# Linear attention, 32 heads: the order of the first and last heads and of the loads, and three stores split unevenly over the DMA engines

## The chip, the cores and the metric

The kernel runs on one core of a Trainium2 chip. The metric is the device time of one execution in microseconds (us), lower is better; where several executions are given it is their median.

A core has five instruction streams: PE (matrix multiplication), DVE (elementwise, reads PSUM and SBUF), ACT (activation functions), POOL (elementwise, SBUF only) and SP (here it only issues DMAs). Sixteen DMA engines carry all transfers between HBM and SBUF. A DMA is split over the engines, and each engine that has done its part adds to the DMA's semaphore.

## The reference

```
phi_q = where(q > 0, q + 1, exp(q)) + 1e-6
phi_k = where(k > 0, k + 1, exp(k)) + 1e-6
kv  = einsum("bhsd,bhse->bhde", phi_k, v)
z   = einsum("bhsd->bhd", phi_k)
num = einsum("bhqd,bhde->bhqe", phi_q, kv)
den = einsum("bhqd,bhd->bhq", phi_q, z)[..., None] + 1e-6
out = num / den
```

q, k, v and out are bfloat16 of shape 1 x 32 x 2048 x 128: 32 heads, each with 512 KB of q, of k, of v and of out, 67.1 MB in all.

## The kernel before

The heads are independent. The 2048 rows of a head lie over 128 partitions, 16 rows (of 128 numbers) to a partition, so that one partition holds 4 KB of a head's q, k, v or out. phi is taken apart as min(exp(x), 1) + 1e-6 plus max(x, 0), and each part has its own matrix multiplication. The steps of head h, by the names that the order lists use (a number behind the point is the part of the head):

- `ldk`, `ldq`, `ldv`: loads into one of seven buffers (`NI = 7`); all are issued by SP but `ldv0`, which ACT issues. A load waits until the steps that read its buffer for head h-7 are done.
- `ek` (ACT) takes exp of k; `em` (DVE) limits it; `rkp` (POOL) is max(k, 0), for half of head 0 `rkd` on DVE. `v1` (POOL) copies v beside a column of ones, so that the sum z comes out of the same multiplication.
- `kv` (PE) is 32 matmuls into one PSUM area; `kvs` (DVE) copies the result to SBUF, and `kv` of the next head waits for that.
- `T` (PE) transposes q into PSUM; `eq` (ACT) takes exp, `emq` (DVE) limits it, `rqa` (ACT) and `rqb` (DVE) take max(q, 0), one half each. There is one PSUM area for the transposes, so `T` of the next head waits for `eq`, `rqa` and `rqb`.
- `n` (PE) multiplies phi_q with kv in two groups of tiles (12 and 4); `r` (DVE) is the reciprocal of the denominator, `f` (DVE) multiplies and writes bfloat16 to one of twelve output buffers (`NO = 12`), `a` (DVE) adds 1e-6 to the denominator of the second group.
- `st` (SP) stores a head, and that of head 31 in three parts. `f` of head h waits for `st` of head h-12, whose buffer it takes.
- `w0` to `w16` are matmuls on the identity matrix without a use of their results, which keep PE busy in the beginning. `ones`, `eps0` to `eps2`, `v1ones0`, `v1ones1` fill constants; `exp` (ACT) runs the activation once.

Nothing is scheduled at run time. Each engine runs its instructions in the order of a list written out by hand (`ORDER`, one string for each engine), and the class `Program` derives from the dependencies which semaphores each instruction waits for. SP's list is therefore also the order in which loads and stores stand in the queue of the DMA engines. An instruction that waits holds up everything behind it in its list.

A load of head 1 and later goes through `wide`, which describes the HBM side as 32 rows of 16 KB; a store goes through `dma_start` with 128 rows (partitions) of 4 KB, so that each of the 16 DMA engines moves 8 rows. The lines of the profile that matter: 344 and 349 loads, 453 stores, 361 `ek`, 364 `em`, 371 `rkp`, 375 `v1`, 382 `kv`, 387 `kvs`, 394 `T`, 398 `eq`, 400 `emq`, 404 `rqa`, 407 `rqb`, 423 and 425 `n`, 438 `a`, 441 `r`, 445 `f`, 330 warm-ups.

Of the kernel before, what the change touches and what calls it, by code (L numbers as in the profile page):

```python
# [6 lines left out]
P = 128  # L7
# [4 lines left out]
NI, NO, NE, NR, NV, NQ, NK = 7, 12, 2, 2, 2, 2, 2  # L12
WARM = (1, 1, 1, 1, 1, 1, 1, 1, 1, 1, 1, 1, 1, 1, 1, 1, 12)
HALVES = ((0, 8), (8, 16))
WHOLE = ((0, 16),)
# [47 lines left out]

def st_parts(h):
    return ((0, 6), (6, 12), (12, 16)) if h == NH - 1 else WHOLE
# [22 lines left out]
def rqb_parts(h):  # L88
    if na(h) == 16:
        return ()  # L90
    if h == NH - 1:
# [6 lines left out]
        w16 w6 w7 w8 w9 w10 w2 T0.0 w0 w11 w12 w5 w13 w1 T0.1 w14 kv0.0 kv0.1 w3 w15 w4 T1.0 kv1.0 n0.0 n0.1  # L98
# [10 lines left out]
        v1ones0 eps0 v1ones1 ones rkd0.0 em0.0 em0.1 emq0.0 em1.0 eps1 rqb0.0 eps2 emq0.1 kvs0 em2.0 kvs1 rqb1.0  # L109
        r0.0 f0.0 emq1.0 em3.0 a0.1 kvs2 r0.1 rqb2.0 f0.1 r1.0 emq2.0 f1.0 em4.0 a1.1 r1.1 rqb3.0 f1.1 r2.0 kvs3  # L110
        f2.0 emq3.0 em5.0 a2.1 r2.1 rqb4.0 f2.1 r3.0 kvs4 f3.0 emq4.0 em6.0 a3.1 r3.1 rqb5.0 f3.1 r4.0 kvs5 f4.0
# [13 lines left out]
        r27.1 rqb29.0 f27.1 r28.0 kvs29 f28.0 emq29.0 em31.0 a28.1 r28.1 rqb30.0 f28.1 r29.0 kvs30 f29.0 emq30.0  # L125
        emq31.0 a29.1 r29.1 emq31.1 f29.1 emq31.2 kvs31 r30.0 f30.0 a30.1 r30.1 f30.1 r31.0 f31.0 a31.1 r31.1
# [12 lines left out]
        ident0 ident rkp0.0 rkp1.0 v10.0 v10.1 v11.0 rkp2.0 v12.0 rkp3.0 v13.0 rkp4.0 v14.0 rkp5.0 v15.0 rkp6.0  # L139
        v16.0 rkp7.0 v17.0 rkp8.0 v18.0 rkp9.0 v19.0 rkp10.0 v110.0 rkp11.0 v111.0 rkp12.0 v112.0 rkp13.0 v113.0  # L140
        rkp14.0 v114.0 rkp15.0 v115.0 rkp16.0 v116.0 rkp17.0 v117.0 rkp18.0 v118.0 rkp19.0 v119.0 rkp20.0 v120.0
        rkp21.0 v121.0 rkp22.0 v122.0 rkp23.0 v123.0 rkp24.0 v124.0 rkp25.0 v125.0 rkp26.0 v126.0 rkp27.0 v127.0
        v128.0 rkp28.0 rkp29.0 v129.0 rkp30.0 v130.0 rkp31.0 v131.0
    """,
    "SP": """
        ldk0.0 ldq0.0 ldk1.0 ldk2.0 ldv1.0 ldq1.0 ldv2.0 ldk3.0 ldq2.0 ldv3.0 ldk4.0 ldq3.0 ldv4.0 ldv5.0 ldq4.0
        ldk5.0 ldk6.0 ldv6.0 ldq5.0 ldq6.0 ldk7.0 ldk8.0 st0.0 ldv7.0 ldv8.0 ldq7.0 ldk9.0 ldv9.0 st1.0 ldv10.0
        ldq8.0 ldk10.0 ldq9.0 ldk11.0 st2.0 ldq10.0 ldq11.0 ldv11.0 st3.0 ldk12.0 ldk13.0 ldv12.0 ldq12.0
        ldv13.0 ldv14.0 ldq13.0 ldk14.0 ldq14.0 ldv15.0 st4.0 ldk15.0 ldv16.0 ldk16.0 ldq15.0 st5.0 ldq16.0
        ldv17.0 ldk17.0 st6.0 ldq17.0 ldv18.0 ldk18.0 st7.0 ldk19.0 ldv19.0 ldq18.0 ldq19.0 st8.0 ldk20.0  # L150
        ldk21.0 ldv20.0 ldk22.0 st9.0 ldq20.0 ldv21.0 ldq21.0 st10.0 ldv22.0 ldk23.0 ldq22.0 ldk24.0 st11.0
        ldv23.0 ldk25.0 ldq23.0 st12.0 ldv24.0 ldq24.0 ldv25.0 st13.0 ldk26.0 ldq25.0 ldv26.0 st14.0 ldk27.0
        ldq26.0 ldv27.0 st15.0 ldk28.0 ldv28.0 ldq27.0 st16.0 ldk29.0 ldq28.0 ldv29.0 st17.0 ldq29.0 ldk30.0
        ldv30.0 st18.0 ldq30.0 ldk31.0 st19.0 ldq31.0 st20.0 ldv31.0 st21.0 st22.0 st23.0 st24.0 st25.0 st26.0
        st27.0 st28.0 st29.0 st30.0 st31.0 st31.1 st31.2
# [13 lines left out]
class Program:  # L169
# [10 lines left out]
    def add(self, eng, key, fn, deps=(), dma=None, inc=True):  # L180
        assert key not in self.op, key
        self.op[key] = (eng, fn, tuple(deps), dma, inc)
# [71 lines left out]
def bass_standalone__linear_attn_elu__prompt_kernel(nc: bass.Bass, q: bass.AP, k: bass.AP, v: bass.AP, out: bass.AP):  # L254
    B, H, S, D = q.shape
    assert D == P and S == 16 * P and B * H == NH
    NT = S // P
# [5 lines left out]
    qf, kf, vf, of = (t.rearrange("b h s d -> (b h) s d") for t in (q, k, v, out))  # L263
    rows = lambda t, h: t[h].rearrange("(p j) d -> p j d", j=NT)

    with ExitStack() as es:
# [70 lines left out]

        def wide(e, to, of):
# [13 lines left out]
        def head(h):  # L352
# [99 lines left out]
            for i, (a, b) in enumerate(st_parts(h)):  # L452
                add("SP", f"st{h}.{i}", lambda e, a=a, b=b: e.dma_start(rows(of, h)[:, a:b], o_sb[:, h % NO, a:b]),
                    [f"f{h}.{j}" for j, (t0, nb, m, b0) in enumerate(groups(h)) if t0 < b and a < t0 + nb * m],
                    dma=f"o{h % NO}")
# [43 lines left out]
```

## Time and profile before

| | |
|---|---|
| median of 3 runs | 169.06 us (169.06 to 169.13) |
| the profiled execution | 169.27 us |
| its span, first to last instruction | 168.0 us |
| mean granted TensorE clock | 0.991 |
| busy: PE, DVE, ACT, POOL | 156.5, 151.9, 149.7, 93.2 us |
| moved by DMA | 67.51 MB, 402 GB/s over the span |
| read from HBM, written | 50.33 MB, 16.78 MB |

The profile comes from one execution. Its time is the span and 1.27 us around it. Times in its rows are counted from the span's start. A row of the timeline reads: start, duration, engine and line, operation, what is written and what is read, how many instructions, and in brackets how long the engine was idle before and what ended that. In the rows of the stretches a busy time stands behind each engine, with the number of instructions in brackets; the DMA share is the mean busy share of the 16 DMA engines. A row of DMA issues ends with the median time from issue to landing. Beside the views, the trace holds every DMA packet (start, duration, bytes, queue; not which of the 16 engines moved it) and the time of every increment of a DMA's semaphore.

### The profile page before, as it was taken

To read this page: it belongs to the slowest core of one execution; us is meant where nothing else is said; L and a number is where in the kernel's file an instruction comes from. 1 tells how busy PE (TensorE), PEld (TensorE's weight loads), DVE (VectorE), ACT (ScalarE), POOL (GpSimd) and SP (SyncE) were. 2 spreads that over 40 slices of the span, in tenths; PEclk is the share of its full clock that TensorE was granted. 3 is DMA by queue.
4 is the path that set the end of the run, shared out by engine and by line. 5 is a ranking of instruction groups with operands and counts; after the bars stand their busy time and mean duration, and the time that the engine had idled before them with its cause. 6 is when DMAs were issued, how large, how long until landed. Compare 5 with 4: busy or idle time off the path is not lost.

```text
span 168.0 us, 6186 instructions
## 1 busy us (share of the span) xinstructions
PE 156.5 (93%) x2716; PEld 150.8 (90%) x2716; DVE 151.9 (90%) x300; ACT 149.7 (89%) x102; POOL 93.2 (55%) x71
## 2 busy tenths in 40 slices
PE   6967999999999999999999999999999989999940
PEld 2456999999999999999999999999999989999840
DVE  0339799999999999999999999999999989999992
ACT  3499899999999999999999999999999979995800
POOL 1397676555555666665555556666655356642000
PEclk9999999999999999999999999999999999999996
DMA  5999999999999999999999999999999999999985
GB/s 207 433 418 414 394 425 386 421 416 410 414 410 425 402 410 396 429 405 431 395 425 419 409 414 430 407 415 419 421 419 423 404 421 436 397 421 409 401 329 216
DMA packets 9819, 67.51 MB, mean 402 GB/s; under 512 B 2080, under 2 KB 2464, under 8 KB 6816
## 3 DMA queue, kind: packets, MB, share of 16 engines
q1 hardware_dynamic: 9648, 66.59, 96.8%
q8 instruction: 21, 0.34, 0.8%
q10 hardware_dynamic: 144, 0.52, 0.8%
q14 instruction: 6, 0.05, 0.1%
HBM read 50.33 MB, written 16.78 MB: 400 GB/s over the span
## 4 chain that ended last, share of the span: by engine, by line
DVE 74%; PE 15%; DMA 4%; issue 3%; ACT 1%; SPq 0%
DVE la L445 36%; DVE la L400 10%; DVE la L364 10%; DVE la L407 9%; PE la L382 7%; DVE la L441 4%; DMA la<-in_k_dram 4%; DVE la L387 3%; PE la L423 3%; PE la L394 3%; PE la L425 3%; DVE la L438 2%; ACT la L361 1%; ACT la L398 1%; SPq L349 0%
## 5 line engine op out<-in xcount | busy, mean ns | idle before, releaser
L371 POOL TENSOR_SCALAR la<-la 128x2048 bf16<-128x2048 bf16 (+1 forms) x32 | 59.9, 1873 | 55.2 <-PE la L382 44.9
L445 DVE TENSOR_TENSOR la<-la 128x1536 bf16<-128x1536 f32 (+2 forms) x65 | 77.7, 1196 | 0.1
L423 PE MATMUL la<-la 128*128 128x129 bf16 x512 | 67.0, 219 | 0.2 <-DVE la L387 0.2
L425 PE MATMUL la<-la 128*128 128x129 bf16 x512 | 67.0, 219 | 0.0
L382 PE MATMUL la<-la 128*128 128x129 bf16 x1024 | 63.3, 220 | 2.0 <-POOL la L375 1.4
L361 ACT ACTIVATE la<-la 128x2048 bf16<-128x2048 bf16 (+1 forms) x33 | 61.3, 1859 | 4.3 <-DMA la<-in_k_dram 4.3
L398 ACT ACTIVATE la<-la 128x2048 bf16<-128x2048 bf16 (+2 forms) x35 | 60.2, 1730 | 4.4 <-PE la L425 2.7
L382 PEld LDWEIGHTS la<-la 128*128 128x128 bf16 x1024 | 59.3, 98 | 2.5 <-issue 1.7
L425 PEld LDWEIGHTS la<-la 128*128 128x128 bf16 x512 | 49.5, 97 | 0.0
L423 PEld LDWEIGHTS la<-la 128*128 128x128 bf16 x512 | 47.9, 97 | 0.4 <-DVE la L387 0.4
L375 POOL COPY la<-la 128x1024 int32<-128x1024 int32 (+1 forms) x33 | 34.1, 1037 | 5.9 <-DMA la<-in_v_dram 5.9
L394 PE MATMUL la<-la 128*128 128x128 bf16 x512 | 34.0, 219 | 1.3 <-DVE la L387 0.9
L404 ACT ACTIVATE la<-la 128x1024 bf16<-128x1024 bf16 (+1 forms) x32 | 33.5, 1046 | 0.0
L394 PEld LDWEIGHTS la<-la 128*128 128x128 bf16 x512 | 29.9, 98 | 2.7 <-DVE la L387 1.0
L400 DVE TENSOR_SCALAR la<-la 128x2048 bf16<-128x2048 bf16 (+2 forms) x35 | 24.0, 687 | 4.5 <-ACT la L398 4.5
L364 DVE TENSOR_SCALAR la<-la 128x2048 bf16<-128x2048 bf16 (+1 forms) x33 | 23.7, 718 | 1.1 <-ACT la L361 1.1
L418 PE MATMUL la<-la 128*128 128x3 bf16 (+1 forms) x128 | 21.6, 168 | 1.3 <-DVE la L445 1.3
L407 DVE TENSOR_SCALAR la<-la 128x1024 bf16<-128x1024 bf16 x31 | 20.5, 661 | 0.0
L441 DVE RECIPROCAL la<-la 128x12 f32<-128x12 f32 (+2 forms) x65 | 13.0, 201 | 1.6 <-PE la L425 0.6
L418 PEld LDWEIGHTS la<-la 128*128 128x128 bf16 x128 | 12.5, 98 | 1.5 <-DVE la L445 1.5
L330 PE MATMUL la<-la 128*128 128x480 bf16 x28 | 7.8, 428 | 1.5 <-POOL la L315 1.5
L387 DVE CAST la<-la 128x129 bf16<-128x129 f32 x32 | 7.7, 240 | 0.8 <-PE la L382 0.8
(16 smaller groups left out, 11.4 us busy)
## 6 DMA issues: line engine op xcount, KB each, us to landing
la<-in_k_dram SPq DMA_DIRECT2D x32, 512.0 KB, 19.6
la<-in_q_dram SPq DMA_DIRECT2D x32, 512.0 KB, 19.7
la<-in_v_dram SPq DMA_DIRECT2D x31, 512.0 KB, 19.6
out_dram<-la SPq DMA_DIRECT2D x31, 512.0 KB, 19.9
la<-in_v_dram ACTq DMA_DIRECT2D x1, 512.0 KB, 5.3
out_dram<-la SPq DMA_DIRECT2D x2, 192.0 KB, 2.7
out_dram<-la SPq DMA_DIRECT2D x1, 128.0 KB, 3.2
```

The lines of the kernel that those rows point to most:

```text
L361: add("ACT", f"ek{h}.{i}", lambda e, a=a, b=b: e.activation(em_sb[:, h % NE, a:b], k_sb[:, h % NI, a:b], ACT.Exp), over("ldk", h, ld_parts ...
L364: add("DVE", f"em{h}.{i}", lambda e, a=a, b=b: e.tensor_scalar(em_sb[:, h % NE, a:b], em_sb[:, h % NE, a:b], 1.0, EPS, op0=ALU.min, op1=AL ...
L371: add("POOL", f"rkp{h}.{i}", lambda e, a=a, b=b: e.tensor_scalar(rk_sb[:, h % NR, a:b], k_sb[:, h % NI, a:b], BIG, 0.0, op0=ALU.min, op1=A ...
L375: add("POOL", f"v1{h}.{i}", lambda e, a=a, b=b: e.tensor_copy(v1_sb[:, h % NV, a:b, 0:D].bitcast(i32), v_sb[:, h % NI, a:b].bitcast(i32)), ...
L382: ins = e.matmul(kv_ps, lhsT=src[:, j], rhs=v1_sb[:, h % NV, j, 0:NC], start=(j + part == 0), stop=(j == NT - 1 and part == 1))
L394: ins = e.transpose(xT[:, j], q_sb[:, h % NI, j], ident[:])
L398: add("ACT", f"eq{h}.{i}", lambda e, a=a, b=b: e.activation(emq_sb[:, h % NQ, a:b], xT[:, a:b], ACT.Exp), over("T", h, t_parts, a, b) + fr ...
L400: add("DVE", f"emq{h}.{i}", lambda e, a=a, b=b: e.tensor_scalar(emq_sb[:, h % NQ, a:b], emq_sb[:, h % NQ, a:b], 1.0, EPS, op0=ALU.min, op1 ...
L407: add("DVE", f"rqb{h}.{i}", lambda e, a=a, b=b: e.tensor_scalar(rq_sb[:, h % NQ, a:b], xT[:, a:b], 0.0, None, op0=ALU.max), over("eq", h, ...
L423: e.matmul(to, lhsT=emq_sb[:, h % NQ, t], rhs=kvs_sb[:, h % NK, 0:NC], start=late and c == 0, stop=False, skip_group_check=True)
L425: ins = e.matmul(to, lhsT=rq_sb[:, h % NQ, t], rhs=kvs_sb[:, h % NK, 0:NC], start=False, stop=True, skip_group_check=True)
L445: return e.tensor_tensor(out=_ap(o_sb[:, :, :, :], first(o_sb[:, h % NO, t0, 0:1]) - first(o_sb[:, :, :, :]), [[m * D, nb], [D, m], [1, D] ...
```

## The change

It has three parts.

1. The lists of PE, DVE and POOL are ordered anew for the first five heads (PE: head 0 and 1 with the warm-ups) and for the last four. For example `kv0.0` goes ahead of `T0.0` on PE, `kvs0` ahead of `emq0.1` on DVE, and `v10.0` ahead of `rkp1.0` on POOL.
2. SP's list is ordered anew throughout: `ldk1` goes ahead of `ldq0`, and fewer stores stand ahead of the last loads (18 of the 32 heads in place of 21).
3. The stores of heads 4, 8 and 17 are taken apart by partitions. Partitions 0 to 95 are stored as before over 16 engines. Partitions 96 to 127 are stored by DMAs whose HBM side has an outermost dimension of 3 or 4: 24 partitions with 3 and 8 with 4 for head 4, 32 with 4 for heads 8 and 17. Between `st4.0`, `st4.1` and `st4.2` stand loads in SP's list; the same holds for `st8.0` and `st8.1`, while `st17.1` follows `st17.0` directly.

The core of the diff:

```
+FEW = {4: ((0, 96, 16), (96, 120, 3), (120, 128, 4)), 8: ((0, 96, 16), (96, 128, 4)), 17: ((0, 96, 16), (96, 128, 4))}
+
+def st_rows(h, i):
+    return FEW[h][i] if h in FEW else (0, P, 16)
+
 def st_parts(h):
+    if h in FEW:
+        return WHOLE * len(FEW[h])
     return ((0, 6), (6, 12), (12, 16)) if h == NH - 1 else WHOLE
...
     "PE": """
-        w16 w6 w7 w8 w9 w10 w2 T0.0 w0 w11 w12 w5 w13 w1 T0.1 w14 kv0.0 kv0.1 w3 w15 w4 T1.0 kv1.0 n0.0 n0.1
+        w16 w2 w0 w6 w7 kv0.0 w8 w5 T0.0 w9 w4 T0.1 w10 w11 w12 w13 w1 kv0.1 w14 w15 w3 T1.0 kv1.0 n0.0 n0.1
...
     "DVE": """
-        v1ones0 eps0 v1ones1 ones rkd0.0 em0.0 em0.1 emq0.0 em1.0 eps1 rqb0.0 eps2 emq0.1 kvs0 em2.0 kvs1 rqb1.0
-        r0.0 f0.0 emq1.0 em3.0 a0.1 kvs2 r0.1 rqb2.0 f0.1 r1.0 emq2.0 f1.0 em4.0 a1.1 r1.1 rqb3.0 f1.1 r2.0 kvs3
-        f2.0 emq3.0 em5.0 a2.1 r2.1 rqb4.0 f2.1 r3.0 kvs4 f3.0 emq4.0 em6.0 a3.1 r3.1 rqb5.0 f3.1 r4.0 kvs5 f4.0
+        ones eps0 em0.0 rkd0.0 v1ones0 em0.1 v1ones1 eps1 em1.0 emq0.0 rqb0.0 kvs0 emq0.1 eps2 em2.0 kvs1 rqb1.0
+        r0.0 f0.0 emq1.0 em3.0 a0.1 kvs2 r0.1 rqb2.0 f0.1 r1.0 f1.0 emq2.0 em4.0 a1.1 r1.1 rqb3.0 f1.1 r2.0 kvs3
+        f2.0 emq3.0 em5.0 a2.1 kvs4 r2.1 rqb4.0 f2.1 r3.0 f3.0 emq4.0 em6.0 a3.1 r3.1 rqb5.0 f3.1 r4.0 kvs5 f4.0
...
-        r27.1 rqb29.0 f27.1 r28.0 kvs29 f28.0 emq29.0 em31.0 a28.1 r28.1 rqb30.0 f28.1 r29.0 kvs30 f29.0 emq30.0
-        emq31.0 a29.1 r29.1 emq31.1 f29.1 emq31.2 kvs31 r30.0 f30.0 a30.1 r30.1 f30.1 r31.0 f31.0 a31.1 r31.1
+        r27.1 rqb29.0 f27.1 kvs29 r28.0 emq29.0 f28.0 em31.0 a28.1 rqb30.0 r28.1 kvs30 f28.1 r29.0 emq30.0 f29.0
+        emq31.0 a29.1 r29.1 f29.1 emq31.1 kvs31 r30.0 emq31.2 f30.0 a30.1 r30.1 f30.1 r31.0 f31.0 a31.1 r31.1
         r31.2 f31.1 f31.2
...
     "POOL": """
-        ident0 ident rkp0.0 rkp1.0 v10.0 v10.1 v11.0 rkp2.0 v12.0 rkp3.0 v13.0 rkp4.0 v14.0 rkp5.0 v15.0 rkp6.0
+        ident0 ident rkp0.0 v10.0 rkp1.0 v10.1 v11.0 rkp2.0 v12.0 rkp3.0 v13.0 rkp4.0 v14.0 rkp5.0 v15.0 rkp6.0
...
-        rkp21.0 v121.0 rkp22.0 v122.0 rkp23.0 v123.0 rkp24.0 v124.0 rkp25.0 v125.0 rkp26.0 v126.0 rkp27.0 v127.0
-        v128.0 rkp28.0 rkp29.0 v129.0 rkp30.0 v130.0 rkp31.0 v131.0
+        rkp21.0 v121.0 rkp22.0 v122.0 rkp23.0 v123.0 rkp24.0 v124.0 rkp25.0 v125.0 rkp26.0 v126.0 v127.0 rkp27.0
+        rkp28.0 v128.0 v129.0 rkp29.0 rkp30.0 v130.0 rkp31.0 v131.0
...
     "SP": """
-        ldk0.0 ldq0.0 ldk1.0 ldk2.0 ldv1.0 ldq1.0 ldv2.0 ldk3.0 ldq2.0 ldv3.0 ldk4.0 ldq3.0 ldv4.0 ldv5.0 ldq4.0
-        ldk5.0 ldk6.0 ldv6.0 ldq5.0 ldq6.0 ldk7.0 ldk8.0 st0.0 ldv7.0 ldv8.0 ldq7.0 ldk9.0 ldv9.0 st1.0 ldv10.0
...
-        ldq26.0 ldv27.0 st15.0 ldk28.0 ldv28.0 ldq27.0 st16.0 ldk29.0 ldq28.0 ldv29.0 st17.0 ldq29.0 ldk30.0
-        ldv30.0 st18.0 ldq30.0 ldk31.0 st19.0 ldq31.0 st20.0 ldv31.0 st21.0 st22.0 st23.0 st24.0 st25.0 st26.0
-        st27.0 st28.0 st29.0 st30.0 st31.0 st31.1 st31.2
+        ldk0.0 ldk1.0 ldq0.0 ldv1.0 ldk2.0 ldq1.0 ldv2.0 ldk3.0 ldq2.0 ldv3.0 ldk4.0 ldq3.0 ldv4.0 ldq4.0 ldk5.0
+        ldv5.0 ldk6.0 ldq5.0 ldv6.0 ldk7.0 ldv7.0 ldv8.0 ldq6.0 ldk8.0 ldq7.0 st0.0 ldv9.0 ldk9.0 ldq8.0 ldv10.0
+        ldk10.0 st1.0 ldk11.0 ldq9.0 ldk12.0 ldq10.0 ldk13.0 ldv11.0 ldq11.0 ldv12.0 ldq12.0 st2.0 ldv13.0
+        ldv14.0 st3.0 ldv15.0 ldk14.0 ldq13.0 st4.0 ldq14.0 ldk15.0 st4.1 ldv16.0 ldk16.0 ldk17.0 ldq15.0
+        ldk18.0 ldq16.0 ldq17.0 ldv17.0 ldk19.0 st4.2 ldq18.0 ldq19.0 ldv18.0 ldv19.0 ldk20.0 st5.0 ldv20.0
+        ldk21.0 st6.0 ldq20.0 ldk22.0 ldq21.0 ldv21.0 ldk23.0 st7.0 ldv22.0 ldk24.0 st8.0 ldq22.0 ldv23.0 st8.1
...
+        ldv27.0 st12.0 ldq27.0 ldv28.0 ldk28.0 st13.0 ldv29.0 ldq28.0 ldk29.0 st14.0 ldq29.0 ldk30.0 st15.0
+        ldv30.0 ldk31.0 ldq30.0 st16.0 ldv31.0 st17.0 st17.1 ldq31.0 st18.0 st19.0 st20.0 st21.0 st22.0 st23.0
+        st24.0 st25.0 st26.0 st27.0 st28.0 st29.0 st30.0 st31.0 st31.1 st31.2
...
+        def some(e, of, to, p0, p1, n):
+            of = of.rearrange("p j d -> p (j d)")[p0:p1]
+            to = to.rearrange("(p j) d -> p (j d)", j=NT)[p0:p1]
+            if n == 16:
+                return e.dma_start(to, of)
+            to = to.rearrange("(n p) e -> n p e", n=n)
+            side = lambda ap, dims: mybir.PhysicalAccessPattern(
+                ap=[list(d) for d in dims], offset=ap.offset, dtype=ap.tensor.dtype, memref=ap.tensor.name,
+                memsetref=ap.tensor.name + "_set", bass_ap=ap)
+            return e.add_instruction(mybir.InstDMACopy(
+                name=nc.get_next_instruction_name(), engine=e.engine,
+                ins=[side(of, [of.ap[0], [NT * D, 1], of.ap[1]])], outs=[side(to, to.ap)],
+                queue="qSPDynamicHW", mode="Copy"))
...
-                add("SP", f"st{h}.{i}", lambda e, a=a, b=b: e.dma_start(rows(of, h)[:, a:b], o_sb[:, h % NO, a:b]),
+                add("SP", f"st{h}.{i}", lambda e, a=a, b=b, i=i: some(
+                    e, o_sb[:, h % NO], of[h], *st_rows(h, i)) if h in FEW else e.dma_start(rows(of, h)[:, a:b], o_sb[:, h % NO, a:b]),
```

In `some`, p0 and p1 are the first partition and the one after the last, and n is the size of the outermost dimension on the HBM side.

## The prediction

> **What bounds the kernel now.** I read the stretches first, to see which resource is full where.
>
> ```profile
> core 0: us, PE busy (x) PEld busy (x) DVE busy (x) ACT busy (x) POOL busy (x), PEclk, DMA share, GB/s
> 0.00:4.00 4.00, 2.48 (x7) 0.99 (x8) 0.28 (x4) 1.49 (x2) 0.70 (x6) 1.00 0.54 195
> 4.00:19.00 15.00, 12.54 (x154) 9.20 (x153) 7.79 (x14) 12.78 (x10) 10.08 (x8) 1.00 1.03 419
> 19.00:135.00 116.00, 115.31 (x2097) 115.13 (x2094) 115.14 (x227) 114.42 (x76) 71.83 (x52) 1.00 1.01 414
> 135.00:155.00 20.00, 19.83 (x358) 19.73 (x359) 19.34 (x37) 17.22 (x12) 10.54 (x8) 1.00 1.01 416
> 155.00:165.00 10.00, 6.29 (x110) 5.77 (x107) 9.33 (x21) 3.77 (x4) 0.00 (x0) 0.99 0.90 361
> ```
>
> Two things are full from 4 to 155 us: the compute engines and all 16 DMA engines. The page's chain of waits names only compute:
>
> ```profile
> ## 4 chain that ended last, share of the span: by engine, by line
> DVE 74%; PE 15%; DMA 4%; issue 3%; ACT 1%; SPq 0%
> ```
>
> The chain follows the last store back to the instruction that released it, so it never asks whether that store stood in a queue. The next two views say that it did.
>
> ```profile
> la<-in_k_dram SPq DMA_DIRECT2D x32, 512.0 KB, 19.6
> ...
> out_dram<-la SPq DMA_DIRECT2D x31, 512.0 KB, 19.9
> ```
>
> ```profile
> 134.53 1.06 SPq L344 DMA_DIRECT2D la<-in_v_dram  x1
> 135.64 29.44 SPq L453 DMA_DIRECT2D out_dram<-la  x13
> ```
>
> A transfer of 512 KB lands 20 us after its issue, although sixteen engines need only 1.25 to 1.28 us for it (landings of consecutive transfers are that far apart in the trace's semaphore events). So some fifteen transfers are always queued. The last load is issued at 134.5 and lands at 153.9; the eleven heads of stores behind it take 11 x 1.27 = 14.0 us, which gives 167.9: where the span ends. The queue sets the end, not DVE, whose last write ends at 164.7.
>
> Which of the sixteen? Each DMA leaves sixteen semaphore increments, one per engine. For head 0's store the last comes 1.75 us after the first, for head 20's store 4.87 us, for head 28's 5.29 us. Sorted, those of head 20 lie at 0, 0.06, 0.21, 0.39, 0.65, 0.83, 1.89, then nine from 3.20 to 4.87 us. The reason stands in the queue table:
>
> ```profile
> q1 hardware_dynamic: 9648, 66.59, 96.8%
> q8 instruction: 21, 0.34, 0.8%
> ```
>
> q8's 21 packets of 16 KB come every 7 us, take about 1.06 us each (0.8% of 16 x 168 us, over 21), and after each of them one increment of the sixteen is some 1.5 us later, for good. By this count nine engines got two or three of them and six got none. The slowest engine has no gap up to its last landing at 167.93, while the five earliest run dry from about 159 us.
>
> **The change, part by part.**
>
> *Rows between engines.* A row is one partition's 4 KB and takes 0.159 us in the trace's record of packets; a whole store puts 8 on each engine. Head 4's store becomes 96 rows over 16 engines (6 each), 24 over three (8 each), 8 over four (2 each); those of heads 8 and 17 become 96 over 16 and 32 over four (8 each). Three engines get 16 + 14 + 14 = 44 rows in place of 24, +20 x 0.159 = +3.18 us; a fourth gets 8 + 14 + 14 = 36, +12 x 0.159 = +1.91 us; twelve get 18, -6 x 0.159 = **-0.95 us**. Each further part costs the engines it uses some 0.05 us (a load's spacing of 1.28 less two packets of 0.611): four more parts on the three engines, 0.2 us, none on the twelve. If the favoured engines are the early ones, the worst of them stands at 0.84 + 3.18 + 0.20 = 4.2 us of lag, the twelve at 5.29 - 0.95 = 4.3. The slowest engine then ends 0.95 us earlier, and nothing else takes its place.
>
> Which engines a three- or four-way transfer takes, this trace cannot show. It has a hint. Head 0's first load starts its sixteen first packets over 228 ns (1.767 to 1.995 us), about 15 ns apiece: engines are served in an order. Head 31's first store starts on five idle, early engines within 59 ns (163.797 to 163.856), so these five are neighbours in that order; and it does so 0.94 us after its issue, against 1.04 us for the first packet of that load, so nothing says that ten others were served before them. Bounds for this term: -0.95 us if the neighbours are the first places, and +1.8 to +3.4 us if the three extra shares fall on engines at 3.2 to 4.9 us of lag. I take the first end.
>
> The Trainium skill states the missing link on its page "DMA: Bandwidth & Descriptors" (why a DMA increments its semaphore by 16): a hardware queue splits over the largest count up to 16 that divides both sides' outer sizes, and uses the lowest-numbered engines. By that the shares are 3 and 4 as the change says; no run here shows it yet.
>
> *A limit behind the engines?* Through the middle the DMA moves 414 GB/s with every engine busy, packets back to back at an unchanged 0.159 us. The same page (Specifications) lists about 358 GB/s as what the HBM gives one core. Were that the binding limit, moving rows between engines would be worth 0; the row is above it, so the row decides.
>
> *Port of the partitions.* The moved rows are all partitions 96 to 127, read by three or four engines, where each engine now reads its own. Nearest rows: 4 KB packets take 0.159 us typically and 0.173 to 0.305 when disturbed near the end. 24 to 32 rows for these engines at up to twice the time would be 3.8 us on engines with no slack; at the undisturbed row, 0. I take 0, nearest to the bulk of packets, and keep +0.5 us in the range.
>
> *Start.* k1 is loaded before q0, so it lands in the slot of 6.96 us in place of 8.20, and q0 in that of 8.20 in place of 6.96. Now ACT reads:
>
> ```profile
> 4.10 2.00 ACT L361 ACTIVATE la<-la 128x1024 bf16<-128x1024 bf16 x2 [1.87 <-DMA la<-in_k_dram]
> 8.22 1.91 ACT L361 ACTIVATE la<-la 128x2048 bf16<-128x2048 bf16 x1 [2.12 <-DMA la<-in_k_dram]
> 10.04 1.92 ACT L398 ACTIVATE la<-la 128x1024 bf16<-128x1024 bf16 x2
> ...
> 20.19 1.88 ACT L398 ACTIVATE la<-la 128x2048 bf16<-128x2048 bf16 x1 [0.84 <-PE la L394]
> ```
>
> ek1 would run 7.0 to 8.85; T0.0 follows q0 at 8.25 and takes 0.62, so eq0 starts at about 9.0 in place of 10.04. POOL converts v10.0 before rkp1.0, and kv0.0 goes ahead of T0.0 on PE in a time when PE only warms (the warm-ups are moved, not dropped). kvs0 goes ahead of emq0.1 on DVE; before, it ended at 15.3 with kv1.0 waiting 0.63 us. That frees T2 earlier and most of the 0.84 us wait. Sum: -1.0 to -1.9 us for head 2 on, I take -1.6. After that heads follow at DVE's and ACT's pace:
>
> ```profile
> 120.78 1.74 DVE L445 TENSOR_TENSOR la<-la 128x1536 bf16<-128x1536 f32 x1
> ...
> 125.40 1.74 DVE L445 TENSOR_TENSOR la<-la 128x1536 bf16<-128x1536 f32 x1
> ```
>
> 4.62 us per head, unchanged.
>
> *Loads and stores reordered.* Before, 21 stores stand ahead of the last load, after only 18, so the last loads land 3 x 1.27 = 3.8 us earlier, plus the 0.95. That removes these waits:
>
> ```profile
> 133.97 1.04 POOL L375 COPY la<-la 128x1024 int32<-128x1024 int32 x1 [2.78 <-DMA la<-in_v_dram]
> ...
> 144.01 1.89 POOL L371 TENSOR_SCALAR la<-la 128x2048 bf16<-128x2048 bf16 x1 [2.56 <-DMA la<-in_k_dram]
> ```
>
> They cost DVE 1.2 us: its long write of head 29 starts at 154.30, where four heads at the pace below, from 134.64 on, would give 153.1. Placing each load of the new order in the landing slots of the old, v4 and v26 come out with no slack and most others with 0.5 to 8 us. The stores' delay is covered by twelve output buffers: store h-12 lands at least 0.6 us before head h writes. If that cover went, DVE would wait about as long as the store is late. SP issues four more DMAs, at 0.33 to 1.05 us each, against 15 to 20 us of queue.
>
> *The last heads* on DVE and POOL swap instructions of 0.1 to 1.9 us among work that waits on PE; bounds -0.5 to +0.5, I take 0.
>
> DVE would then end near 164.7 - 1.6 - 1.2 = 161.9, and its last store could land by about 164. All that is spare: behind the 18th store still stand 14 heads of stores, 17.8 us of queue. **Sum:** span 168.0 - 0.95 = 167.05; with 1.27 us around it (169.27 less 168.0) 168.3 for a profiled execution, and 169.06 - 0.95 = **168.1** for the median, which lies 0.2 below the profiled one. The compute gain of 2.8 us is bought twice and paid once.
>
> **Rivals.** *The chain is right* and compute sets the end: 169.06 - 2.8 = 166.3. Against it, the slowest engine's bytes less 0.95 us end at 167.0 whatever DVE does; even perfect balance of head 28's lags (mean 2.7, last 5.3) allows only -2.6. *Wrong engines* (slower): the three-way shares fall on engines that served instruction packets. With a lag of 3.2 + 3.4 against 4.9 the end moves +1.7, with 4.9 + 3.4 +3.4: 170.8 to 172.5, and loads are late on top. It decides as soon as a favoured engine's lag is above 1.5 us (4.9 less 3.4). *The shares do not arrive*: the 32 rows spread over sixteen anyway, or their port gives back what is moved. Then four parts of 0.05 us are left, or the gain of 0.95 less up to 1: 168.9 to 169.3.
>
> **How the numbers follow.** Forecast 0.70, compute sets the end 0.04, wrong engines 0.13, shares lost 0.13. A measurement here can tell 0.2%, 0.34 us. The forecast's own spread is 167.7 to 168.6 (start and port); all but its tails and the compute rival are faster: 0.72. Shares lost and the tail are the same: 0.13. Wrong engines and the rest: 0.15. For 8 in 10 the range is 167.7 to 169.4, which leaves out the wrong engines and the lowest rival.
>
> **What would show it.** In the after profile, the 4 KB q1 packets stay at 0.159 us; the spread between first and last increment of the late stores falls from 5 us to about 1.5; v31 lands before 150; POOL's waits on loads near the end vanish; ACT's wait of 0.84 at 20 us goes; DVE ends near 162 and the span near 167.0, with DMA full to the end. A spread that grows to 7 us says wrong engines; a spread unchanged at 5 says that the shares did not arrive; an end that follows DVE's by 2 us says that compute ruled.

## The result, and the profile after

| | before | after |
|---|---|---|
| median | 169.11 us (20 runs, 168.96 to 169.48) | 168.75 us (20 runs, 168.52 to 169.27) |
| ratio | | 0.9979, 95% interval 0.9970 to 0.9988 |
| profiled execution, its span | 169.27, 168.0 us | 168.74, 167.4 us |
| DVE's last write ends | 164.7 us | 163.6 us |
| last load (v31, q31) landed | 153.9 us | 149.3 us |

The change gains 0.36 us where 0.96 was forecast (168.1). That is 0.2% and clear of the noise, and 168.75 lies inside the range of 167.7 to 169.4, but little more than a third of the forecast gain came.

The stretches of the profiled execution after, columns as before:

```profile
core 0: us, PE busy (x) PEld busy (x) DVE busy (x) ACT busy (x) POOL busy (x), PEclk, DMA share, GB/s
...
19.00:135.00 116.00, 114.03 (x2071) 113.65 (x2069) 115.14 (x225) 113.05 (x75) 72.25 (x51) 1.00 1.01 413
135.00:155.00 20.00, 20.00 (x367) 20.00 (x365) 19.90 (x38) 18.05 (x13) 9.96 (x7) 1.00 1.02 416
155.00:165.00 10.00, 5.17 (x90) 4.64 (x87) 8.12 (x20) 2.99 (x4) 0.00 (x0) 1.00 0.96 388
165.00:168.00 3.00, 0.00 (x0) 0.00 (x0) 0.00 (x0) 0.00 (x0) 0.00 (x0) 0.76 0.30 109
```

DMA is full to 155 us as before, and fuller from 155 to 165 (0.96; 0.90 before): some of the engines that had run dry now work nearly to the end. In the last row nothing but DMA works. The page's chain of waits has changed:

```profile
## 4 chain that ended last, share of the span: by engine, by line
PE 88%; DVE 8%; issue 0%; POOL 0%; POOLq 0%
```

It was DVE 74%, and not one DMA is in it now, although the queue is as long as before. Nor does the chain go with the time: in two kernels below it reads PE 88% at 169.29 us (the new order alone) and DVE 74% at 168.77 us (the split alone). The issues by line, and SP's last ones in time (a row of several issues has the time from the first to the last):

```profile
la<-in_k_dram SPq DMA_DIRECT2D x32, 512.0 KB, 19.2
...
out_dram<-la SPq DMA_DIRECT2D x28, 512.0 KB, 19.2
out_dram<-la SPq DMA_DIRECT2D x3, 384.0 KB
```

```profile
127.95 1.06 SPq L351 DMA_DIRECT2D out_dram<-la  x1
129.05 0.69 SPq L356 DMA_DIRECT2D out_dram<-la  x1
...
130.70 33.26 SPq L477 DMA_DIRECT2D out_dram<-la  x16
```

Lines 351 and 356 are the two parts of head 17's store, the 96 partitions and the four shares. Behind them stand fourteen heads of stores, as the prediction counted. The late waits for loads are gone from POOL:

```profile
146.84 1.89 POOL L394 TENSOR_SCALAR la<-la 128x2048 bf16<-128x2048 bf16 x1 [1.74 <-PE la L405]
148.68 1.49 POOL L398 COPY la<-la 128x1024 int32<-128x1024 int32 x1
```

Before, the last two such rows waited for the loads of k31 (2.24 us) and v31 (2.94 us, until it landed at 153.9); now PE sets the pace. The rows of before:

```profile
149.13 1.89 POOL L371 TENSOR_SCALAR la<-la 128x2048 bf16<-128x2048 bf16 x1 [2.24 <-DMA la<-in_k_dram]
153.96 1.04 POOL L375 COPY la<-la 128x1024 int32<-128x1024 int32 x1 [2.94 <-DMA la<-in_v_dram]
```

**Did the shares arrive?** Yes, and on the forecast engines. The 24 partitions of head 4 over three engines leave three semaphore increments, at 69.15, 69.16 and 69.23 us. The 32 partitions of head 8 over four engines leave four, from 106.84 to 107.40. The load ahead of head 4's three shares, k15, has its first five increments from 67.85 to 67.97, and the next at 68.14; 8 rows of 0.159 later is 69.12 to 69.24, so the three engines are among the five earliest of the sixteen. That fits the rule which the prediction took from the Trainium skill ("DMA: Bandwidth & Descriptors", why a DMA increments its semaphore by 16: the lowest-numbered engines). The trace shows how many engines took part and that they were early ones; it does not number them. The 4 KB packets keep their 0.159 us, so the port of the moved partitions gave nothing back.

**Where the gain went.** The last increment of a late store tells when the slowest engine has done it:

| store of head | before | after | difference |
|---|---|---|---|
| 27 | 162.80 | 161.80 | -1.00 |
| 28 | 164.20 | 163.09 | -1.11 |
| 29 | 165.37 | 164.41 | -0.96 |
| 30 | 166.62 | 166.13 | -0.49 |
| 31, last data packet | 167.46 | 166.99 | -0.47 |

Until 164.4 us the whole forecast 0.95 was there; in the last two microseconds half of it was lost. At the end fifteen engines had finished by 166.44 us, and one alone worked on to 166.99. So two questions are left: is it the split that brings the 0.95 (and not order or compute), and what holds that one engine back.

### The profile page after: what moved, and what is told of

The parts are those of the page before. It is cut to its first block, busy times and chain, and to the rows that moved or that the text cites. A ratio compares the mean times of both kernels' runs of the same rounds, so it can differ in the third digit from the quotient of the medians.

```text
span 167.4 us, 6190 instructions
## 1 busy us (share of the span) xinstructions
PE 156.7 (94%) x2716; PEld 151.2 (90%) x2716; DVE 154.4 (92%) x300; ACT 149.5 (89%) x102; POOL 94.1 (56%) x71
## 4 chain that ended last, share of the span: by engine, by line
PE 88%; DVE 8%; issue 0%; POOL 0%; POOLq 0%
PE la L405 34%; PE la L446 17%; PE la L417 17%; PE la L448 16%; PE la L339 5%; DVE la L468 4%; DVE la L387 1%; DVE la L423 1%; DVE la L464 1%; DVE la L430 0%; PE la L441 0%; DVE la L461 0%; DVE la L410 0%; POOL la L324 0%; POOL la L323 0%
## 5 line engine op out<-in xcount | busy, mean ns | idle before, releaser
L387 DVE TENSOR_SCALAR la<-la 128x2048 bf16<-128x2048 bf16 (+1 forms) x33 | 24.8, 751 | 6.1 <-ACT la L384 6.1
L423 DVE TENSOR_SCALAR la<-la 128x2048 bf16<-128x2048 bf16 (+2 forms) x35 | 25.1, 717 | 0.3 <-ACT la L421 0.3
L339 PE MATMUL la<-la 128*128 128x480 bf16 x28 | 8.8, 464 | 1.5 <-POOL la L324 1.5
```

What stands on the lines that cost most here:

```text
L423: add("DVE", f"emq{h}.{i}", lambda e, a=a, b=b: e.tensor_scalar(emq_sb[:, h % NQ, a:b], emq_sb[:, h % NQ, a:b], 1.0, EPS, op0=ALU.min, op1 ...
```

## Experiments: which part brings the gain

Theory A is the prediction's: the slowest DMA engine sets the end. Theory B is its first rival: compute sets the end, and the new order gains. Three kernels on one chip, beside 35 runs of before with a median of 169.12.

**Order alone** (all new lists, no store taken apart):

```diff
-FEW = {4: ..., 8: ..., 17: ...}
+FEW = {}
-    ... st4.1 ... st4.2 ... st8.1 ... st17.1 ...
```

> The new order of all lists, the three stores whole again (four DMAs fewer). Theory A (the DMA engine with the most bytes and instruction packets sets the end): the end does not move against the kernel before, 169.1 us, ratio 0.999 to 1.002, DVE ends near 163.6 and the slowest engine's last landing near 168.0. Theory B (earlier loads and the new order of heads bring the gain): the whole gain, 168.75, ratio 0.998.

Measured: 169.29 us, ratio 1.0014 (1.0005 to 1.0023), span of the profiled execution 167.8, DVE's end 163.4.

**Split alone** (all lists of before, the parts directly behind each other):

```diff
-    "SP": ... st4.0 ... st8.0 ... st17.0 ...
+    "SP": ... st4.0 st4.1 st4.2 ... st8.0 st8.1 ... st17.0 st17.1 ...
```

> The old order of all lists, the three stores split (the parts directly behind one another in SP's list). Theory A: the slowest engine is relieved by six rows, 0.95 us; the end moves by the measured gain of the whole change or more, ratio 0.994 to 0.998, and DVE ends between 163.8 and 164.7, since the loads land up to 0.95 us earlier. Theory B: no gain, ratio 0.999 to 1.001.

Measured: 168.77 us, ratio 0.9981 (0.9972 to 0.9989), span 167.5, DVE's end 164.0.

**After once more**, the same kernel on that chip:

> The changed kernel again, beside the other runs on this chip. Both theories: 168.75 us, ratio 0.997 to 0.999. In the profile, if the one engine that ended 0.55 us behind the others is a matter of chance, it ends elsewhere or not at all; if it belongs to the program, one engine again ends about 0.5 us behind a pack of eight to ten.

Measured: 168.75 us (168.41 to 169.39), ratio 0.9981 (0.9971 to 0.9991). This profiled execution took 168.41, its span is 167.1, DVE ended at 161.95, and no engine stood alone at the end (the last one finished at 166.68, the one before it less than 0.1 us earlier).

What follows: the split brings the whole gain, the order nothing; alone it even costs 0.17 us, for which I found no cause. Theory B is excluded. The two profiles of after make it plain: DVE ended 1.65 us earlier in the second, and over all runs the kernel is no faster than the split alone.

**One store cut short**, to price the queue:

```diff
-FEW = {4: ..., 8: ..., 17: ...}
+FEW = {4: ..., 8: ..., 17: ..., 20: ((0, 16, 16),)}
```

> After's kernel, but of head 20's store only the first 16 partitions are written, so that 112 rows of its output stay unwritten and every engine has seven rows less (7 x 0.159 = 1.11 us). Theory A, the slowest engine's rows set the end: 168.75 - 1.11 = 167.6. If anything else (the last heads on DVE, SP's issues) stood close behind the queue, less comes out: DVE's end at 163.6 plus about 2 us for the last store allows an end of 165.7 where the queue would end at 165.9, so nothing else should show. Theory B, compute sets the end: 168.75.

Measured: 167.78 us (6 runs) against 169.16 of before, ratio 0.9917 (0.9904 to 0.9931): 0.97 below after's 168.75. The profiled span is 166.0; its last stretch:

```profile
165.00:168.00 3.00, 0.00 (x0) 0.00 (x0) 0.00 (x0) 0.00 (x0) 0.00 (x0) 0.57 0.07 23
```

Seven rows less on every engine take away about what seven rows cost (1.11), with no compute work touched. The end moves with the rows on the slowest engine.

## Experiments: how much of it, by dose

If each moved row counts, a kernel with fewer or more moved rows should follow the line. After's lists, other splits:

```diff
 one store
+FEW = {8: ((0, 96, 16), (96, 128, 4))}
 two stores
+FEW = {8: ((0, 96, 16), (96, 128, 4)), 17: ((0, 96, 16), (96, 128, 4))}
 a light third
+FEW = {4: ((0, 112, 16), (112, 128, 4)), 8: (as above), 17: (as above)}
 four stores
+FEW = {4: (as in after), 8: (as above), 12: ((0, 96, 16), (96, 128, 4)), 17: (as above)}
```

> After's lists, but of the three stores only that of head 8 is taken apart (96 partitions over 16 engines, 32 over four). Theory A, the slowest engine sets the end and each moved store takes two rows (0.32 us) off it: 169.29 (order alone) - 0.32 = 168.97, favoured engines about 2.5 us ahead of the slowest at the end, spread from run to run as small as before's. Theory C, a late disturbance of about 0.45 us costs any version with moved rows the same whatever their number: 169.4. Theory D, the four favoured engines in after stand beside the slowest and any disturbance of theirs moves the end: the same 168.97 here, since they are far ahead.

> After's lists, with the stores of heads 8 and 17 taken apart, that of head 4 whole. Theory A: 169.29 - 0.64 = 168.65, favoured engines some 1.2 us ahead of the slowest. Theory C: 169.1. Theory D, the favoured engines cost after 0.3 to 0.4 us of its gain: 168.65, as fast as after (168.75) or faster although it moves a third less, and a smaller spread from run to run than after's 168.4 to 169.4.

> After's lists, with the stores of heads 8 and 17 taken apart as in after, and of head 4's store only 16 partitions (112 to 127) over four engines, so that each of the four gets three rows more and each of the twelve one row less. Theory A: 169.29 - 0.64 - 0.16 = 168.49, favoured engines some 0.6 us ahead of the slowest. Theory C: 168.95. Theory D: 168.5, faster than after by 0.25 us.

> After's lists, and the store of head 12 taken apart as well (96 over 16, 32 over four), so that the favoured engines get six rows more (0.95 us) and the twelve others two less. They stood within 0.1 us of the slowest in after. Theories A and D: the favoured engines set the end, 0.95 - 0.1 = 0.85 us after after's: 169.5 to 169.6, last landing by three or four engines alone, and a large spread from run to run. Theory C, only a late disturbance matters: 168.75 - 0.32 = 168.4.

And, from the first batch, after with a ladder of shares on top, to see which places the early engines hold:

```diff
+FEW = {4: ..., 8: ..., 17: ..., 20: ((0, 96, 16), (96, 104, 8), (104, 111, 7), (111, 117, 6), (117, 122, 5), (122, 126, 4), (126, 128, 2))}
```

> The changed kernel, and the store of head 20 taken apart too: 96 partitions over 16 engines, then 8, 7, 6, 5, 4 and 2 partitions over as many engines, one row each. The landings of the small parts tell which lag the first 2, 4, 5, 6, 7 and 8 engines have at that time. If the lowest places belong to the engines without instruction packets, the first seven land within about 2 us of the earliest engine, the eighth may be 3 us or later. Time: the engines beyond the eighth lose another 2 rows, 0.32 us. Theory A: 0.1 to 0.3 us less than the changed kernel, if the six small parts cost the first engines no more than 0.05 us each; Theory B: no change against it.

Measured (before: 169.12 and 169.16 on the two chips):

| kernel | rows taken from each of twelve | forecast from order alone | store 27's last increment | its change | median | ratio |
|---|---|---|---|---|---|---|
| order alone | 0 | | 162.69 | | 169.29 | 1.0014 |
| one store | 2 | -0.32 | 162.36 | -0.33 | 169.06 | 0.9991 (0.9982 to 1.0000) |
| two stores | 4 | -0.64 | 162.12 | -0.57 | 169.00 | 0.9994 (0.9980 to 1.0007) |
| light third | 5 | -0.80 | 162.06 | -0.63 | 169.31 | 1.0011 (1.0001 to 1.0022) |
| after, two profiles | 6 | -0.95 | 161.80, 161.89 | -0.89, -0.80 | 168.75 | 0.9979 |
| four stores | 8 | favoured engines last | 162.72 | +0.03 | 169.99 | 1.0049 (1.0031 to 1.0067) |

The ladder took 169.53 us (169.08 to 171.31), ratio 1.0043 (1.0018 to 1.0068). I had expected a small gain from it; it gives the four favoured engines three or four rows and five or six parts more than after does, and they already stood close to the slowest (an estimate follows in the account of the prediction). Its increments told what it was for. Up to 149 us head 20's parts leave four increments (147.99, 148.05, 148.20, 148.46), the next comes at 151.03. Had an early engine held one of the places five to seven, it would have left at least two small increments more in that time; one more than three early engines leave by themselves fits the eighth place, which gets a single row. So of the places behind the first four only the eighth belongs to an early engine, and two more early engines lie beyond it. So no share over the first n engines reaches them without loading full ones, and the split of after is about as far as this device goes. Four stores say the same: three engines at the top (162.48 to 162.72 us), the last 0.9 us later than after's at store 27.

Up to four microseconds before the end the line is followed: 0.13 to 0.17 us per row, against 0.159 (one profile each; after's two lie 0.09 us apart). The medians do not follow it. A light third should be near the best and is the slowest of those with fewer than four stores. Theory D (the favoured engines themselves spoil after) falls: in the kernels with one and two stores the favoured engines are 1.3 us or more ahead, and the medians still fall short by 0.1 to 0.35. Theory C as it was stated, one fixed loss for every version, misses too: it asked for 169.4, 169.1, 168.95 and 168.4, and 169.06, 169.00, 169.31 and 169.99 came. What is left is a looser form of it: something that happens late, in some kernels and some executions. The profiled executions with one and two stores are among the fastest of theirs (168.78 and 168.65, where theory A asked for 168.97 and 168.65), and no engine stands alone at their end. In the light third, as in after, one engine ended alone: the others had finished by 166.80 us, it worked on to 167.40.

## Experiments: the packet that hits one engine

The queue table of after has the candidate, and it stood in before's table too:

```profile
q1 hardware_dynamic: 9663, 66.59, 97.3%
q8 instruction: 21, 0.34, 0.8%
...
q14 instruction: 6, 0.05, 0.1%
```

q14 carries 8 KB packets of instructions. The last of the six starts at 163.97 us in before, 164.06 in after, 162.75 in the light third. It takes 0.309 us, and in after and the light third the two rows behind it (each starts where the one ahead ended, so I take them to be on the same engine) take 0.37 and 0.30 to 0.31 instead of 0.159: together some 0.67 us more than two plain rows take, a lag behind the others that this engine never makes up. In the light third all engines stood within one tight pack at store 27 (the last two at 4.72 and 4.73 us behind the first), and at store 30, after the packet, one stood 0.71 us behind the rest (5.19 and 4.48).

If so, the lone engine must move with the packet. Whose instructions are they? DVE's and SP's streams were made longer by 24 waits on a condition that is always met:

```diff
     def emit(self, eng, engine):
+        keys = ORDER[eng].split()
+        for at, (fn, waits, name, by) in enumerate(self.plan[eng]):
+            if keys[at] in MORE.get(eng, ()):
+                for _ in range(12):
+                    engine.wait_ge(self.get("POOL"), 1)
```

In the expectations from here on e2 is the split alone, e7 the light third, e9 the light third with DVE's waits, and e13 and e16 are after and the split alone with twelve additions moved to PE.

On DVE ahead of `em1.0` and `em2.0`, in the light third's kernel:

> The kernel of e7, with 24 waits on a condition long met put into DVE's list (twelve ahead of em1.0, twelve ahead of em2.0, where DVE has idle time), so that DVE's later instructions stand 24 places further on. Theory C': the lone engine that ended 0.6 us behind the pack in e7 was hit by the 8 KB instruction packet of 162.7 us, and that packet belongs to DVE's stream: it comes some 8 to 10 us earlier, or lands elsewhere, and the outlier is gone or sits in a different engine: about 168.5 to 168.8 in place of 169.3. If the packet belongs to another stream it stays near 162.7 and the time stays at 169.3. Theory E, the outlier has nothing to do with that packet: 169.3 whatever the packet does.

On SP ahead of `st11.0` and `st12.0`, in the light third's kernel:

> The kernel of e7, with 24 such waits in SP's list (twelve ahead of st11.0, twelve ahead of st12.0; SP runs 15 us ahead of the queue there). Theory C' with SP as the packet's owner: the packet of 162.7 us moves by several us (earlier) and the outlier with it: 168.5 to 168.8; with another owner: nothing moves, 169.3. Theory E: 169.3 in either case.

On DVE in after's kernel:

> After's kernel with the 24 waits of e9 in DVE's list. Theory C' with DVE as owner: the packet of 164.06 us moves to about 155, so it falls on another engine or at least before the end; the median moves towards the undisturbed 168.4, or away from it if it falls on one of the pack in every run: 168.4 to 168.9. Other owner, or theory E: 168.75 as before, within 0.1.

| kernel | DVE's packets (us) | store 24: last two increments behind the first | last two engines end at | median | ratio |
|---|---|---|---|---|---|
| light third | 35.2, 104.5, 162.7 | 4.76, 4.77 | 166.80, 167.40 | 169.31 | 1.0011 |
| its SP + waits | 35.1, 104.5, 162.9 | 4.85, 4.89 | 166.74, 167.34 | 169.19 | 1.0008 (1.0000 to 1.0017) |
| its DVE + waits | 30.9, 101.4, 157.0 | 4.74, 5.87 | 166.70, 167.70 | 169.32 | 1.0020 (1.0007 to 1.0032) |
| after, DVE + waits | 29.4, 99.5, 155.2 | 4.70, 5.43 | 166.54, 167.15 | 168.98 | 0.9993 (0.9982 to 1.0005) |

Three of the six packets are DVE's, the late one among them: these three come 3 to 6 us earlier with a longer DVE stream in the light third, and with a longer SP stream all six stay within 0.6 us. The lone engine moves too. With the packet at 155 to 157 us it stands behind the pack already at store 24; with the packet at 163 it does so only after. In time I was wrong: I had hoped that an earlier packet might fall elsewhere. It fell on one of the pack again, and a lag once taken stays.

The Trainium skill ("Runtime: NRT & Kernel Launch", instruction fetch mechanics) says that each engine's sequencer fetches its next page of instructions through a DMA queue of its own, 16 KB at a time, and that the cost is mostly hidden. For DVE it is: the profile has no wait of DVE that it would explain. For the DMA engine that carries the page it is not, and here the DMA engines set the end; and the pages on q14 are 8 KB, those on q8 16 KB.

## Experiments: without the packet

The last test is a kernel in which DVE's last page is not fetched. DVE's stream was made shorter: for some heads PE starts the denominators of the second group with 1e-6, as it does for the first group, and DVE's addition `a` goes away.

```diff
 def eps_dve(h, i):
-    return i == 1
+    return i == 1 and h not in range(10, 22)
...
-    ... a10.1 ... a21.1 ...
```

Twelve heads, in after, in the light third, in before, and in the split alone:

> After's kernel with twelve instructions less in DVE's stream: for heads 10 to 21 the addition of 1e-6 to the second group's denominators (a) is left to PE, which starts these sums with a small multiplication, as it does for the first group. Theory C', DVE's last 8 KB instruction packet (163 to 164 us) costs most runs of after 0.5 to 0.7 us: with twelve places less DVE reaches its end before the place at which that packet is fetched, the packet is gone or comes after the end, and the median falls to 168.4 (before less 0.7), with a small spread. If the packet still comes (the end of the stream reaches over the place), 168.75 as before. Theory E, something else takes the gain: 168.75 though the packet is gone.

> The kernel of e7 (16 partitions of head 4's store over four engines), with the same twelve additions left to PE. Theory C': 169.3 falls to 168.5 if the packet is gone. Theory E: 169.3.

> Control: the kernel before, with the same twelve additions left to PE. Its late packet fell on an engine with over 1 us in hand, and the slowest engine is another: theory C' 169.1, no change. If this were a matter of compute time or of PE's and DVE's pace (theory B), it would change by as much as the others do.

> The split alone (old lists, e2, 168.77) with the same twelve additions left to PE. Theory C': 168.77 falls to 168.4 or less if the packet is gone, the lowest of all versions with whole output. Theory E: 168.77.

The same with 24 heads (`range(5, 29)`), in after and in the split alone:

> After's kernel with 24 additions (heads 5 to 28) left to PE in place of twelve. If the 0.24 us around the span are the instruction packet that DVE now waits for behind its last work, twelve places more take it away: span 167.0 to 167.1 again, around it 1.30, median 168.3 to 168.4. If those 0.24 us belong to the edit itself or to something that 24 places don't reach: 168.6 as in e13. PE's added multiplications (24 x 2, some 0.06 us each) make DVE end about 1 us later, near 163, still ahead of the queue.

> The split alone (old lists) with 24 additions left to PE. Fetch theory: span 167.0, around it 1.30, median 168.3. Otherwise 168.56 as in e16. Here DVE ends later (164.3 in e16, about 164.6 now), so that its last store could land by 166.6: just ahead of the queue's end at 166.7, and any more would show.

The packet is gone, in all six. The queue table and the last stretches of after with 24 additions on PE:

```profile
q1 hardware_dynamic: 9663, 66.59, 97.6%
q8 instruction: 21, 0.34, 0.8%
...
q14 instruction: 5, 0.04, 0.1%
```

```profile
155.00:165.00 10.00, 4.21 (x73) 3.69 (x69) 7.36 (x18) 2.03 (x2) 0.00 (x0) 0.98 0.96 389
165.00:168.00 3.00, 0.00 (x0) 0.00 (x0) 0.00 (x0) 0.00 (x0) 0.00 (x0) 0.50 0.30 111
```

Five packets on q14 where there were six. DMA carries as much in the last three microseconds as in after (0.30), but many engines end together: the last seven between 166.48 and 166.58 us.

| kernel | median | ratio | median span | time around it |
|---|---|---|---|---|
| before | 169.09 | | 167.8 | 1.30 |
| before, 12 on PE (control) | 169.41 | 1.0020 (1.0012 to 1.0029) | 167.9 | 1.53 |
| after | 168.75 | 0.9979 (0.9970 to 0.9988) | 167.4 | 1.32 |
| after, 12 on PE | 168.60 | 0.9971 (0.9961 to 0.9981) | 167.0 | 1.55 |
| split alone, 12 on PE | 168.56 | 0.9968 (0.9955 to 0.9980) | 167.0 | 1.54 |
| light third, 12 on PE | 168.97 | 1.0007 (0.9989 to 1.0025) | 167.4 | 1.55 |
| after, 24 on PE | **168.31** | 0.9959 (0.9947 to 0.9971) | 167.0 | 1.32 |
| split alone, 24 on PE | 168.44 | 0.9961 (0.9948 to 0.9974) | 167.0 | 1.39 |

(The time around the span is the mean of a run's time less its span.) Without the packet the median span of after and of the split alone falls to 167.0: 0.8 us below before's 167.8, of the 0.95 that was forecast, where after with the packet has 0.4. The control, with twelve, shows that the edit by itself does not shorten the span: 167.9 against 167.8. Before with 24 was not run. After and before with the same edit are 168.60 and 169.41, 0.81 us apart where the plain kernels are 0.36 apart; for the split alone it is 0.85. Seven of the eight runs of after with twelve on PE lie between 168.50 and 168.66, where after's go from 168.4 to 169.4.

My expectation for twelve missed one thing: 0.24 us appear around the span, in the control too, and with 24 they go away (1.32) or mostly so (1.39). That fits a page that DVE still needs behind its last work when its stream ends just short of the place, and no longer needs when it ends well short; the trace does not show what lies outside the span, so this is argued and not shown.

After with 24 additions on PE is the fastest kernel here that writes its whole output: 168.31 us against 169.14 of before on the same chip, 0.83 us less.

Not settled: what picks the DMA engine that carries a page. In after's two profiles it hit the pack once and once not; in the light third's kernel, with and without the waits, it hit in all three profiles, and none of 35 runs was below 169.06. The light third without the packet has runs in two groups (seven from 168.69 to 169.03, four from 169.56 to 170.13), and its median stays 0.37 above after's with the same edit, 0.5 above its forecast of 168.5; for that I have no cause. Single late runs also remain in after without the packet (one of eight at 169.06, with the last engine 0.21 us behind the rest, and one of eleven at 169.31), so the packet is not the only late disturbance.

## Why the prediction was right and wrong

*What bounds the kernel*: right. Order alone, split alone and the store cut short all say that the slowest DMA engine ends the kernel and that DVE's end does not matter.

*Rows between engines, -0.95*: the term is about right at the place where it acts (-0.89 and -0.80 from order alone, -1.00 from before, at store 27), as is the choice of engines and the port at 0. The prediction had the favoured engines 0.1 us ahead of the slowest, and the four-store kernel agrees: there they have six rows and one part more, about 1.0 us by the prediction's prices, and the last three engines reach the end of store 27 at 162.48 to 162.72. Less 1.0 that is some 161.5 to 161.7 in after, where the slowest has 161.80 (an estimate; the traces do not name the engines). So there was nothing left to move.

*"The slowest engine then ends 0.95 us earlier, and nothing else takes its place"*: this is the step that failed. Something else does take its place: an engine that carries DVE's last page of instructions. In the median span that cost 0.4 us (0.4 gained with the packet, 0.8 without); the rest of the missing gain, about 0.15 us, fits the row term itself, which came out at 0.80 to 0.89. I had counted q8's 21 packets and put q14's six, at 0.1% of the queue's time in the same table, at nothing without a reason. More than that, I took the end to be one engine's. Before, one engine led the end by a little and only five stood near it, so the packet could fall on an engine with time in hand. In before's profile it did: the last six engines keep their distances to one another from store 29 to store 30, and the others stand over 1 us ahead of the last. Levelled, nine or ten engines stand within 0.3 us, and a late delay of 0.5 to 0.7 us on any of them is the end. Of twelve profiles of kernels with moved rows and that packet, seven have one engine alone by 0.5 to 1.0 us at the end; of the five such kernels without it none has more than 0.21.

*Start, -1.6, and the late loads, -1.2*: in the second profile of after DVE's long write of head 2 starts at 26.81 us, against 28.42 before, which is -1.61, and DVE ends at 161.95, as forecast (161.9). In the first it starts at 28.60 and DVE ends at 163.60. The 2.3 us won at head 0 (16.80 against 19.11) were lost again within two heads. DVE of the first profile, and POOL in the same time:

```profile
16.80 1.76 DVE L468 TENSOR_TENSOR la<-la 128x1536 bf16<-128x1536 f32 x1
18.48 1.51 DVE L423 TENSOR_SCALAR la<-la 128x2048 bf16<-128x2048 bf16 x1
19.90 2.37 DVE L387 TENSOR_SCALAR la<-la 128x2048 bf16<-128x2048 bf16 x1
```

```profile
18.40 1.04 POOL L398 COPY la<-la 128x1024 int32<-128x1024 int32 x1 [1.22 <-DMA la<-in_v_dram]
19.74 1.99 POOL L394 TENSOR_SCALAR la<-la 128x2048 bf16<-128x2048 bf16 x1 [0.31 <-PE la L405]
```

The same two DVE instructions in the second profile, where POOL had no wait for that load and stood idle from 18.85 to 20.45:

```profile
19.18 0.68 DVE L423 TENSOR_SCALAR la<-la 128x2048 bf16<-128x2048 bf16 x1
19.78 0.68 DVE L387 TENSOR_SCALAR la<-la 128x2048 bf16<-128x2048 bf16 x1
```

In the first, DVE's 3.9 us in place of 1.4 hold up `rqb` and with it the next transposes on PE, and ACT behind them:

```profile
23.26 1.07 PE L417 MATMUL la<-la 128*128 128x128 bf16 x16 [1.59 <-DVE la L430]
```

```profile
6.70 1.91 ACT L384 ACTIVATE la<-la 128x2048 bf16<-128x2048 bf16 x1 [0.73 <-DMA la<-in_k_dram]
8.99 1.94 ACT L421 ACTIVATE la<-la 128x1024 bf16<-128x1024 bf16 x2 [0.38 <-PE la L417]
...
24.82 1.88 ACT L421 ACTIVATE la<-la 128x2048 bf16<-128x2048 bf16 x1 [2.20 <-PE la L448]
```

ek1 at 6.70 and eq0 at 8.99 are where the prediction put them (7.0 and 9.0). The wait of 0.84 us at 20 us is gone, and one of 2.20 stands at 24.8. As the prediction held, none of this reaches the end: the two executions differ by 1.65 us at DVE's end and by 0.33 in time, and nearly all of that is the lone engine's (last data packets at 166.99 and 166.68).

*The spread of the late stores* was to fall to 1.5 us and stayed near 4.8 (store 27: 4.76, 5.12 before). I had reckoned with all seven early engines. The shares reach four; three stay over 2.5 us ahead of everybody and run dry as before. The slowest engine is no worse for that, so the sum was not touched. But the sign that I had named for it was wrong: a spread unchanged at 5 was to say that the shares did not arrive, and they did.

*Rivals*: compute sets the end (166.3) and the wrong engines (170.8 to 172.5) are excluded by the kernels above. "The shares do not arrive" named a time next to the measured one (168.9 to 169.3), but by another way: they arrived in full.

## What to carry to other kernels

Here a full DMA queue ended with its slowest engine, and the chain of waits did not show it: read the sixteen increments of the late transfers. Work can be moved between the DMA engines by the outer dimension of a transfer, but once they are level, a late disturbance of any of them can become lost time, so look for what else uses these engines near the end, above all instruction pages, and get it out of the way too. A forecast for the maximum of many nearly equal things must hold a term for the disturbance, not only the mean.

## What the runs showed of the hardware

- A page of instructions costs the DMA engine that carries it a lag that stays: some 0.67 us by the packets for DVE's last 8 KB packet (the lone engines ended 0.5 to 1.0 us behind the rest), some 1.4 to 1.5 us for q8's 16 KB. Twelve or 24 instructions less in a stream of some 320 took the last page away.
- 128x2048 bf16 instructions on DVE took 0.68 us with POOL idle, and 1.51 and 2.37 us while POOL ran. Those that started ahead of POOL's instruction and overlapped it kept 0.69 us (at 26.25 us in after, where POOL starts at 26.68).
- One engine's 4 KB rows take 0.17 to 0.19 us in stores where the others take 0.159, so that it falls back by 0.13 to 0.16 us per store. In before's profile it seems to be the last of all (the last engine falls back by such steps); in after's first profile the one with the packet ended behind it. The Trainium skill ("DMA: Bandwidth & Descriptors", latency and other measured facts) calls engines 7 and 15 usually slower and ties its best guess at the cause to DMAs issued by GpSimd. This kernel issues none there; the trace shows one slower engine all the same and cannot name it.
